# One kernel of attention and two expert layers: the hand-over order of its first phase written anew

## The chip, the cores and the metric

The kernel runs on one core of a Trainium2 chip. The metric is the device time of one execution in microseconds (us); lower is better. The core has five engines that each take their own instructions in order: TensorE (PE, with its weight loads as PEld), VectorE (DVE), ScalarE (ACT), GpSimd (POOL) and SyncE (SP), which here only issues transfers from HBM. They meet through semaphores.

## The reference, cut to what matters

Three stages follow one another: two kinds of attention that are added, then a mixture of 8 experts where each token goes to one, then a dense layer with a clipped quadratic in the middle.

```python
# q, k, v: (4, 8, 576, 64) float32
q_d, k_d, v_d = (a.reshape(B, H, 144, 4, D).mean(axis=3) for a in (q, k, v))
out_up = np.repeat(softmax(scale * q_d @ k_d.T) @ v_d, 4, axis=2)
mask = np.abs(pos[:, None] - pos[None, :]) < 4
out_local = softmax(np.where(mask, scale * q @ k.T, -1e9)) @ v
x = (out_up + out_local) as (2304, 512)
e = argmax(x @ w_gate)                 # one expert for each token
x = gate * (relu(x @ w1[e]) @ w2[e])   # (512 -> 1024 -> 512)
h = x @ w_in                           # (512 -> 2048)
out = where(h >= 1, h, where(h <= -1, 0, (h + 1)**2 / 4)) @ w_out
```

## The kernel before, in words

The first phase, up to about 120 us, computes both attentions for the four batches, the gating and the place of each token, and scatters the token rows into a buffer ordered by expert. The expert layer and the dense layer follow; they are the same in both kernels.

The first phase is a list of 526 short steps in the string `ORDER`. A loop walks it once and calls a function for each word, so the order of the words is the order in which every engine and the transfer queue get their instructions:

```python
    for step in ORDER.split():
        name, *args = step.split(".")
        ...
            fn, dve, other = CHOICE[name[:2]]
            ...
            fn(dve if name[2] == "v" else other, *args)
```

A word is a step and its indices. Where a third letter stands it chooses the engine: `v` is DVE, `p` POOL, `a` ACT. The steps that the prediction speaks of:

- Loads, all issued by SP in the order of the words: `q.b.i` (batch b of q in two pieces of 128x4x200 and 128x4x384 float32, 400 KB and 768 KB), `kr.b` (k for the pooled attention, 128x4x576, 1152 KB), `kb.n` (half a batch of k for the local attention), `vs.U` (v, 512 KB), `cs` (constants, 160 KB and 137 KB). A `kb` load is two transfers of 64x1184 (296 KB each) into 64 of the 128 partitions, into one of three buffers `kbd`, whose other quarters are zeroed by the memsets `mk`.
- Local attention, in 12 units U, three to a batch: `S.U` (scores on PE: one mask product, then 32 small float32 products, which the trace shows as 64 weight loads and 64 matmuls), `mx` and `sb` (row maximum, and its subtraction, on DVE), `ex` (exponential, ACT), `sm` (sum and reciprocal, DVE), `nm` (normalize, DVE or POOL), `tr` (transpose, DVE), `bd` (copies into a block layout `at`), `AV.U.g` (product with v, PE), `ac`/`ad`/`ap` (result into xT). `ma` zeroes the two `at` buffers.
- Pooled attention, batch by batch: `ka` and `pq` (pooling of k and q), `SD` (scores), `dm`, `dn`, `de`, `ds`, `dx` (softmax), `TD` (transposes on PE, copied into `adT` by `tc`), `vp` and `vc` (pooled v), `VD` (product), `vo`.
- Gating: `lg`, `ct`, `ch`, `ra`, `rk`, `rd` (logits, choice, place), `xt` and `xm` (rows transposed back and scaled by the gate), `xs` (scatter).
- `wu.i`: two products of 128x512 of ones by ones on PE, whose results nobody reads.

The functions of the half-partition load and of the scores:

```python
    def ld_kb(n):
        ...
        for h in range(2):
            SP.dma_start(out=kb[64 * h:64 * h + 64, h], in_=kT[b, x, 64 * h:64 * h + 64])
```

Of the kernel before, what the change touches and what calls it, by code (L numbers as in the profile page):

```python
# [56 lines left out]


ORDER = """
kr.0 mav.0 q.0.0 kap.0.0 m1 mkp.0.1 wu.0 wu.1 mkp.0.0 wu.2 mkv.1.1 wu.3 cs.0 q.0.1 kb.1 pqv.0.0 kap.0.1 ci mkp.2.0  # L60
pqv.0.1 kb.0 wu.4 mkv.1.0 q.1.1 wu.5 cm q.1.0 wu.6 me mdv.1 wu.7 S.0 SD.0.0 SD.0.1 cf wu.8 mx.0 wu.9 mkp.2.1 sb.0
wu.10 wu.11 wu.12 wu.13 S.1 dm.0.0.1 kr.1 mdv.0 dm.0.1.0 kb.2 dm.0.0.0 kb.3 dm.0.1.1 ex.0 vs.0 dn.0 cs.1 pqp.1.0 sm.0
nmv.0 wu.14 mx.1 tr.0 S.2 de.0.1.0 wu.15 kav.1.0 S.3 de.0.0.1 vs.1 pqp.1.1 de.0.1.1 mx.2 kap.1.1 sb.2 de.0.0.0 sb.1
ds.0 mx.3 SD.1.1 dm.1.1.1 ex.2 SD.1.0 dxp.0 bda.0.2 sb.3 dm.1.0.0 bda.0.3 dm.1.1.0 dm.1.0.1 ex.1 map.1 S.5 bda.0.0
sm.2 kb.4 TD.0.1 vs.2 sm.1 nmp.2 mx.5 bda.0.1 ex.3 dn.1 de.1.1.1 de.1.0.0 AV.0.0 tcv.0.1 TD.0.2 de.1.1.0 S.4 tca.0.2
AV.0.1 de.1.0.1 nmp.1 sm.3 tr.1 mx.4 tr.2 TD.0.0 bda.1.1 bdv.1.2 vp.0.0 acv.0.1 vp.0.1 q.2.0 aca.0.0 bdv.2.3 ds.1 cr
S.6 bda.1.0 bda.1.3 sb.4 kb.5 TD.0.4 mx.6 q.2.1 vca.0.0 kr.2 nmp.3 dxp.1 TD.0.3 ex.4 sb.5 AV.1.1 aca.1.1 sm.4 vca.0.1
AV.1.0 wg tca.0.3 bda.2.2 vs.4 TD.1.3 bda.2.1 vs.5 tcv.0.4 tr.3 tca.0.0 bda.2.0 aca.1.0 TD.1.1 nmv.4 bda.3.1 sb.6 vs.3
TD.1.4 pqv.2.0 VD.0.1 bdv.3.2 VD.0.0 TD.1.0 pqp.2.1 ex.5 TD.1.2 tr.4 tca.1.1 tca.1.4 AV.2.1 ex.6 AV.2.0 S.8 tca.1.0
sm.5 bda.3.0 tca.1.2 voa.0.0 kav.2.0 kav.2.1 acv.2.1 SD.2.0 bda.4.0 bdv.4.2 voa.0.1 tca.1.3 ce sm.6 bda.3.3 SD.2.1  # L70
mx.8 ap.1.0 ap.0.0 vp.1.1 bda.4.1 bda.4.3 vca.1.1 nmv.5 aca.2.0 dm.2.0.0 AV.3.1 aca.3.1 ap.0.1 ap.1.1 AV.3.0 tr.5
bda.5.0 nmp.6 S.7 lg.0 dm.2.1.0 dm.2.0.1 kr.3 sb.8 dm.2.1.1 mx.7 vp.1.0 aca.3.0 lov.0 ct.0 kb.6 dn.2 de.2.0.1 tr.6
de.2.1.1 vca.1.0 bdv.5.3 sb.7 AV.4.1 bdv.5.1 kav.3.0 de.2.1.0 AV.4.0 xt.2 xt.1 ap.2.1 ch.0 kav.3.1 de.2.0.0 ds.2 ra.0
VD.1.1 aca.4.0 vov.1.1 cx.0 dxv.2 xt.0 VD.1.0 ex.7 rk.0 kb.7 q.3.0 bda.5.2 q.3.1 gt.0 S.9 bdv.6.0 voa.1.0 TD.2.3
bda.6.1 aca.4.1 xma.0 rd.0 tca.2.3 AV.5.0 xma.2 ap.2.0 TD.2.2 TD.2.1 AV.5.1 sm.7 mx.9 ck acv.5.1 bda.6.3 ap.4.0
aca.5.0 pqp.3.0 pqp.3.1 S.10 SD.3.0 ex.8 ap.5.0 bda.6.2 vs.6 xs.0 ap.3.1 xma.1 tca.2.1 sm.8 TD.2.0 SD.3.1 mx.10
tca.2.2 AV.6.1 vs.7 nmv.7 ap.4.1 sb.9 dm.3.0.0 dm.3.1.0 S.11 dm.3.0.1 vs.8 ap.3.0 tr.7 ex.9 aca.6.1 dm.3.1.1 tca.2.0
dn.3 TD.2.4 vs.10 lg.1 sb.10 de.3.1.0 vp.2.1 loa.1 bdv.7.0 de.3.0.0 sm.9 ct.1 xs.2 vs.9 vp.2.0 ch.1 ra.1 tca.2.4
vcv.2.1 de.3.1.1 cx.1 bdv.7.3 ap.5.1 mx.11 bda.7.2 bdv.7.1 lg.2 vca.2.0 gt.1 nmp.8 loa.2 xt.5 AV.6.0 xt.3 aca.6.0 rk.1
tr.8 rd.1 xt.4 xma.5 de.3.0.1 xma.3 nmv.9 ct.2 VD.2.1 sb.11 bda.8.3 ch.2 ex.10 vp.3.0 tr.9 xs.1 xs.5 ds.3 xma.4  # L80
bda.8.1 ra.2 cx.2 bdv.8.0 xt.7 vs.11 xt.6 dxv.3 rk.2 vov.2.1 xs.3 VD.2.0 AV.7.1 vp.3.1 vov.2.0 vca.3.1 xs.4 AV.7.0
bda.8.2 gt.2 ad.7.1 xmv.6 sm.10 ap.6.1 TD.3.1 TD.3.0 xma.7 TD.3.2 ad.7.0 tca.3.1 ex.11 vca.3.0 AV.8.0 TD.3.4 rd.2
tcv.3.2 bda.9.0 tca.3.4 ap.6.0 lg.3 tca.3.0 bda.9.3 lov.3 nmp.10 xt.8 bdv.9.2 VD.3.0 xma.8 ad.8.0 tr.10 bda.9.1 ra.3
TD.3.3 AV.8.1 sm.11 ct.3 xs.6 voa.3.0 ad.8.1 tca.3.3 xs.7 AV.9.0 xs.8 VD.3.1 bda.10.1 bda.10.0 ch.3 bda.10.2 bda.10.3
nmv.11 voa.3.1 xt.10 cx.3 gt.3 aca.9.0 ap.9.0 AV.9.1 xt.9 rk.3 xt.11 tr.11 AV.10.0 aca.9.1 ap.9.1 rd.3 lg.4 xma.10
AV.10.1 xmv.9 ad.10.0 bda.11.0 xma.11 bdv.11.2 bdv.11.1 loa.4 bda.11.3 ct.4 ra.4 xs.10 ad.10.1 ch.4 cx.4 xt.12 xt.13
lg.5 rk.4 gt.4 xs.11 AV.11.1 AV.11.0 rd.4 xs.9 xma.13 loa.5 ad.11.1 ct.5 ad.11.0 xt.14 ch.5 lg.6 ra.5 xma.12 loa.6
xma.14 ct.6 rk.5 rd.5 xs.13 xt.15 cx.5 ra.6 ta gt.5 xt.17 xs.12 xs.14 xma.15 xt.16 ch.6 xs.15 cx.6 gt.6 rk.6 rd.6
xma.16 xma.17 tb xs.16 st ps xs.17
"""  # L90


# [1185 lines left out]
```

## Time and profile before

| | us |
|---|---|
| median of 3 runs | 760.63 (759.74 to 762.31) |
| the profiled execution's own time | 763.32 |
| its span in the profile | 761.5 |
| TensorE busy in the span | 729.6 |
| VectorE busy in the span | 524.0 |

The profile is of one execution. Its span runs from the first instruction to the last; the time of that execution is 1.8 us longer than the span. Busy time is the time in which an engine had an instruction in work.

### The profile page before, as it was taken

What the parts mean: (1) busy time and instruction counts of PE and PEld (TensorE: products, weight loads), DVE (VectorE), ACT (ScalarE), POOL (GpSimd) and SP (SyncE); (2) the same over time, 40 slices, a digit from 0 to 9 for tenths busy, and PEclk for the clock granted to TensorE, in tenths of its full rate; (3) what the DMA queues carried; (4) which work ended last, traced back from release to release, by engine and by line L of the source; (5) the groups of instructions that cost most, each with busy time, mean ns of one, the idle gap of its engine ahead of it and who ended that gap; (6) DMA issues with size and microseconds to landing.
All of it is one profiled execution on the core that took longest, in us unless ns stands there. A gap on an engine that the chain in (4) does not pass through costs nothing.

```text
span 761.5 us, 14260 instructions
## 1 busy us (share of the span) xinstructions
PE 729.6 (96%) x5520; PEld 655.9 (86%) x5521; DVE 524.0 (69%) x891; ACT 339.5 (45%) x697; POOL 254.2 (33%) x240
## 2 busy tenths in 40 slices
...
GB/s 284 248 235 318 113 86 185 261 210 177 143 209 202 200 217 246 202 174 51 29 55 28 56 56 28 57 29 56 28 56 28 56 0 1 1 42 41 42 42 83
DMA packets 47816, 87.09 MB, mean 114 GB/s; under 512 B 3084, under 2 KB 23948, under 8 KB 47736
## 3 DMA queue, kind: packets, MB, share of 16 engines
...
## 4 chain that ended last, share of the span: by engine, by line
PE 81%; issue 6%; DVE 4%; DMA 4%; POOL 2%; ACT 1%; SPq 1%; POOLq 0%; ACTq 0%; DVEq 0%
PE s L1065 24%; PE y L1163 15%; PE s L1003 13%; PE y L1020 13%; PE o L1163 8%; DMA kbd<-in_dram 2%; POOL out_dram L1183 1%; PE o L963 1%; DMA q_t<-in_dram 1%; PE o L400 1%; DMA xs_d<-xr,dst_all 1%; DMA xr<-xs_d 1%; PE s L400 1%; PE y L400 1%; PE o L524 1%
## 5 line engine op out<-in xcount | busy, mean ns | idle before, releaser
L1065 PE MATMUL s<-yT,wh 128*128 128x384 f32 x448 | 141.5, 339 | 0.0
L906 POOL TENSOR_SCALAR cvm<-cvm 128x512 f32<-128x512 f32 x32 | 52.9, 1654 | 243.9 <-ACT cvm L905 243.5
L1077 ACT CAST hh<-r 128x384 fp32r<-128x384 f32 x95 | 48.7, 513 | 161.0 <-DVE r L1073 161.0
L1072 DVE SCALAR_TENSOR_TENSOR r<-r 128x384 f32<-128x384 f32 x96 | 61.7, 643 | 64.9 <-ACT r L1071 63.7
L178 DVE TENSOR_TENSOR wl<-wraw,wh 128x1024 fp32r<-128x1024 f32 x64 | 82.2, 1303 | 22.5 <-ACT wh L177 22.0
L1071 ACT ACTIVATE r<-s,half 128x384 f32<-128x384 f32 x96 | 55.8, 581 | 87.9 <-PE s L1065 87.5
L1078 DVE TENSOR_TENSOR hl<-r,hh 128x384 fp32r<-128x384 f32 x95 | 56.4, 594 | 55.1 <-ACT hh L1077 53.9
L1065 PEld LDWEIGHTS s<-yT,wh 128*128 128x128 f32 x448 | 83.5, 188 | 4.8
L1065 PE MATMUL s<-yh,wh 128*128 128x384 f32 x256 | 85.9, 335 | 0.0
L1065 PE MATMUL s<-yh,wl 128*128 128x384 f32 x256 | 85.3, 333 | 0.0
L881 POOL TENSOR_TENSOR wl<-cvm,wh 128x512 fp32r<-128x512 f32 x32 | 50.8, 1587 | 99.7 <-ACT wh L880 88.7
L1163 PE MATMUL y<-wl,hh 128*128 128x512 f32 x189 | 74.1, 392 | 0.0
L1163 PE MATMUL y<-wh,hh 128*128 128x512 f32 x189 | 73.8, 391 | 0.0
L1020 PE MATMUL y<-hh,wh 128*128 128x240 f32 (+5 forms) x256 | 72.4, 303 | 0.0
L177 ACT CAST wh<-wraw 128x1024 fp32r<-128x1024 f32 x64 | 65.6, 1046 | 15.1 <-DMA wraw<-in_dram 10.6
L1020 PE MATMUL y<-hh,wl 128*128 128x240 f32 (+5 forms) x256 | 71.2, 298 | 0.0
L949 ACT ACTIVATE hh<-s 128x416 fp32r<-128x416 f32 (+7 forms) x64 | 27.9, 436 | 78.7 <-PE s L1003 78.7
L1163 PE MATMUL y<-wh,hl 128*128 128x512 f32 x189 | 59.5, 394 | 0.0
L950 DVE SCALAR_TENSOR_TENSOR hl<-s,hh 128x416 fp32r<-128x416 f32 (+7 forms) x64 | 31.1, 486 | 39.9 <-ACT hh L949 39.6
L1073 DVE TENSOR_TENSOR r<-s,r 128x384 f32<-128x384 f32 x96 | 53.5, 557 | 3.3
L1065 PEld LDWEIGHTS s<-yh,wh 128*128 128x128 f32 x256 | 48.0, 188 | 2.7
L1020 PEld LDWEIGHTS y<-hh,wl 128*128 128x128 f32 x256 | 48.3, 189 | 0.0
...
## 6 DMA issues: line engine op xcount, KB each, us to landing
...
```

The source lines that it names most:

```text
L177: ACT.copy(out=hi, in_=raw)
L178: DVE.tensor_tensor(out=lo, in0=raw, in1=hi.bitcast(F32), op=ALU.subtract)
L881: POOL.tensor_tensor(out=lo, in0=m, in1=hi.bitcast(F32), op=ALU.subtract)
L906: POOL.tensor_scalar(out=m, in0=m, scalar1=PAT_MIN * PAT_MIN, scalar2=None, op0=ALU.is_ge)
L1003: PE.matmul(out=h_ps[:, 0:m], lhsT=w[wi][:, o:o + 128], rhs=xhl[c][xi][:, 0:m], start=(n == 0), stop=(n == 11))
L1020: PE.matmul(out=y_ps[c][:, 0:m], lhsT=w[wi][:, o:o + 128], rhs=hl[xi][:, 0:m], start=(f == 0 and i == 0), stop=(f == 7 and i == 1))
L1065: PE.matmul(out=h_ps[:, 0:CAP], lhsT=w[wi][:, o:o + 128], rhs=yhl[j, c][xi], start=(n == 0), stop=(n == 11))
L1071: ACT.activation(out=r, in_=h_ps[:, 0:CAP], func=AF.Relu, scale=0.5, bias=half[:, 0:1])
L1072: DVE.scalar_tensor_tensor(out=r, in0=r, scalar=1.0, in1=r, op0=ALU.min, op1=ALU.mult)
L1073: DVE.tensor_tensor(out=r, in0=h_ps[:, 0:CAP], in1=r, op=ALU.max)
L1078: DVE.tensor_tensor(out=lo[:, 0:CAP], in0=r, in1=hi[:, 0:CAP].bitcast(F32), op=ALU.subtract)
L1163: PE.matmul(out=p, lhsT=gl[gi][:, 128 * t:128 * t + 128], rhs=w[wi][:, o + c:o + c + p.shape[-1]], start=(f % 4 == 0 and i == 0), stop=(f ...
```

## The change

Only the string `ORDER` changes: 521 words in place of 526, in another order, and with other engine letters on some. Sixteen `wu` words become eleven. Everything else is word for word the same, one line higher in the file (the string is a line shorter).

```diff
 ORDER = """
-kr.0 mav.0 q.0.0 kap.0.0 m1 mkp.0.1 wu.0 wu.1 mkp.0.0 wu.2 mkv.1.1 wu.3 cs.0 q.0.1 kb.1 pqv.0.0 kap.0.1 ci mkp.2.0
...
+mkv.2.1 m1 mkv.1.1 wu.0 mav.0 q.0.0 mdv.0 mkv.0.1 kb.0 wu.1 mkp.0.0 wu.2 cs.0 ci mav.1 cm S.0 q.0.1 me wu.3 mkv.2.0
...
```

The transfer queue (SP) at the start of the program, before. `kbd_100`, `kbd_101` and `kbd_102` are the three buffers of half-partition loads; `x2` is the pair of one `kb` step:

```order
L273 DMA kraw<-in_dram 128x4x576
L268 DMA q_t<-in_dram 128x4x200
L259 DMA cs<-in_dram 128x320
L268 DMA q_t<-in_dram 128x4x384
L287 DMA kbd_101<-in_dram 64x1184 x2
L287 DMA kbd_100<-in_dram 64x1184 x2
L268 DMA q_t<-in_dram 128x4x384
L268 DMA q_t<-in_dram 128x4x200
L273 DMA kraw<-in_dram 128x4x576
L287 DMA kbd_102<-in_dram 64x1184 x2
```

The same queue in the changed kernel:

```order
L267 DMA q_t<-in_dram 128x4x200
L286 DMA kbd_100<-in_dram 64x1184 x2
L258 DMA cs<-in_dram 128x320
L267 DMA q_t<-in_dram 128x4x384
L272 DMA kraw<-in_dram 128x4x576
L286 DMA kbd_101<-in_dram 64x1184 x2
L267 DMA q_t<-in_dram 128x4x200
L286 DMA kbd_102<-in_dram 64x1184 x2
L267 DMA q_t<-in_dram 128x4x384
L286 DMA kbd_100<-in_dram 64x1184 x2
```

The first `kraw` goes from first to fifth place, and the first pair of `kbd` from sixth to second; the second `kraw` stands behind all ten.

VectorE at the start of the program, before. `at_98` and `adp_109` are work buffers that are zeroed, `pt` and `qd` the pooling of q, `mx` the first row maximum:

```order
L302 MEMSET at_98 128x2048
L305 MEMSET kbd_101 64x1184
L452 TENSOR_TENSOR pt<-q_t 128x1152
L455 TENSOR_TENSOR qd<-pt 128x576
L305 MEMSET kbd_101 64x1184
L299 MEMSET adp_109 128x60x8
L367 TENSOR_REDUCE mx<-s_171 128x16
L371 TENSOR_TENSOR a_103<-s_171,mx 128x16x32
```

The same engine in the changed kernel:

```order
L304 MEMSET kbd_102 64x1184
L304 MEMSET kbd_101 64x1184
L301 MEMSET at_98 128x2048
L298 MEMSET adp_108 128x60x8
L304 MEMSET kbd_100 64x1184
L301 MEMSET at_99 128x2048
L304 MEMSET kbd_102 64x1184
L366 TENSOR_REDUCE mx<-o_136 128x16
L370 TENSOR_TENSOR a_103<-o_136,mx 128x16x32
L277 TENSOR_TENSOR kraw<-kraw 128x1152
L280 TENSOR_TENSOR k_d<-kraw 128x576
L304 MEMSET kbd_101 64x1184
```

Memsets moved here from POOL, the pooling of q went to POOL, and the first pooling of k (`kraw`, `k_d`) came from POOL.

TensorE from the scores of unit 5 on (`S.5`, `TD`, `AV`, `TD`, `S.4`, `AV`), before:

```order
L359 MATMUL y_441<-kbd_100,q_t 32x64 x32
L503 MATMUL s_481<-ident,adp_108 96x128 x4
L400 MATMUL y_503<-at_98,v_s 64x96 x8
L503 MATMUL y_514<-ident,adp_108 96x128 x4
L350 LDWEIGHTS identb
L350 MATMUL s_521<-maskb,identb 128x512
L359 MATMUL s_521<-kbd_102,q_t 32x64 x16
L359 MATMUL s_521<-kbd_100,q_t 32x64 x16
L400 MATMUL o_556<-at_98,v_s 64x96 x8
```

The same piece of work in the changed kernel, from `S.2` on (`S.2`, `S.5`, `S.4`, `AV`, `TD`, `vp`, `TD`, `AV`):

```order
L358 MATMUL y_359<-kbd_101,q_t 32x64 x32
...
L358 MATMUL y_393<-kbd_100,q_t 32x64 x32
L349 LDWEIGHTS identb
L349 MATMUL o_433<-maskb,identb 128x512
L358 MATMUL o_433<-kbd_102,q_t 32x64 x16
L358 MATMUL o_433<-kbd_100,q_t 32x64 x16
L399 MATMUL y_474<-at_98,v_s 64x96 x8
L502 MATMUL s_486<-ident,adp_108 96x128 x4
L410 MATMUL y_491<-v_s,cs 32x512 x3
L502 MATMUL o_506<-ident,adp_108 96x128 x4
L399 MATMUL s_519<-at_98,v_s 64x96 x8
```

Three scores now stand next to one another, with no transposes or products between them, and the scores of the second batch's pooled attention (`SD.1`), which stood ahead of `S.5`, stand behind all of this.

## Rows read from the trace of the kernel before

**Rows 1.** Busy time by stretch: stretch, its length, busy (instructions) by engine, PEclk, DMA, GB/s.

```profile
18.00:33.50 15.50, 14.34 (x378) 9.15 (x376) 14.90 (x29) 11.01 (x43) 10.63 (x7) 1.00 1.02 291
33.50:45.00 11.50, 8.16 (x139) 4.89 (x139) 5.42 (x13) 5.21 (x16) 4.07 (x3) 0.70 0.75 214
45.00:84.00 39.00, 38.65 (x754) 27.68 (x751) 37.21 (x76) 31.86 (x90) 21.30 (x23) 1.00 0.73 243
84.00:118.80 34.80, 32.84 (x470) 24.97 (x468) 26.81 (x88) 23.06 (x53) 19.76 (x31) 1.00 0.30 108
...
134.60:761.50 626.90, 620.54 (x3662) 582.01 (x3662) 425.71 (x653) 263.45 (x488) 184.96 (x148) 1.00 0.29 94
```

**Rows 2.** The chain that ended last, 30 to 60 us: start, length, what.

```profile
33.52 3.34 issue
36.86 1.29 PE s L359 x37
...
40.64 1.81 PE o L411 x6
...
46.48 0.66 PE o L400 x16
...
48.58 1.18 PE y L524 x16
...
56.53 1.02 PE y L411 x6
```

**Rows 3.** DVE's waits, 20:40 and 40:64: total, times, longest.

```profile
DVE mx L367 <- PE s L359: 3.0, 1, 3.0
...
DVE mx L367 <- PE y L359: 2.9, 1, 2.9
```

**Rows 4.** Busy time from 0 (columns as rows 1); instruction queue at 34.0:34.5 and 0:38.5.

```profile
0.00:29.30 29.30, 18.91 (x356) 10.32 (x357) 19.32 (x28) 9.36 (x33) 15.78 (x22) 1.00 0.96 289
...
0.00:33.50 33.50, 23.11 (x473) 13.38 (x474) 23.42 (x37) 13.06 (x48) 19.98 (x25) 1.00 0.97 284
...
q8 instruction: 1, 0.02, 13.8%
...
q8 instruction: 4, 0.07, 0.8%
```

**Rows 5.** Busy time, while full-width loads run and while half-partition loads run.

```profile
4.00:8.00 4.00, 0.00 (x0) 0.00 (x0) 0.27 (x1) 0.00 (x0) 1.58 (x1) 1.00 1.07 382
11.00:15.00 4.00, 4.00 (x11) 1.38 (x10) 3.66 (x3) 0.00 (x0) 3.80 (x9) 1.00 1.01 230
```

**Rows 6.** The timeline, first instructions: start, length, what, [idle before <-releaser].

```profile
1.28 1.76 DVE L302 MEMSET at<- 128x2048 f32 x1 [1.16 <-PEq L1266]
...
6.42 2.61 POOL L278 TENSOR_TENSOR kraw<-kraw 128x1152 f32<-128x1152 f32 x1 [5.55 <-DMA kraw<-in_dram]
...
16.98 0.69 DVE L367 TENSOR_REDUCE mx<-s 128x16 f32<-128x512 f32 x1 [1.20 <-PE s L359]
...
25.95 1.10 PE L359 MATMUL y<-kbd,q_t 128*32 128x64 f32 x64 [0.96 <-DMA kbd<-in_dram]
```

**Rows 7.** DVE by line and form, 0 to 119 us: busy, mean ns, idle before.

```profile
L385 DVE TENSOR_TENSOR a<-a,sm 128x512 f32<-128x512 f32 x6 | 4.5, 752 | 0.0
...
L278 DVE TENSOR_TENSOR kraw<-kraw 128x1152 f32<-128x1152 f32 x3 | 4.0, 1321 | 0.0
...
L452 DVE TENSOR_TENSOR pt<-q_t 128x1152 f32<-128x1152 f32 x2 | 2.7, 1350 | 6.3 <-DMA q_t<-in_dram 6.3
L305 DVE MEMSET kbd<- 64x1184 f32 x2 | 2.1, 1045 | 0.5 <-issue 0.5
...
L701 DVE TENSOR_SCALAR xr<-s,gt 128x512 f32<-128x512 f32 x1 | 0.7, 742 | 0.0
...
L512 DVE COPY adT<-y 96x512 f32<-96x512 f32 x1 | 0.7, 677 | 0.0
...
L514 DVE COPY adT<-o 96x256 f32<-96x256 f32 x1 | 0.4, 356 | 0.0
```

More of the change, by code (lines that the diff above doesn't have):

```diff
@@ L59 @@
 ORDER = """
-kr.0 mav.0 q.0.0 kap.0.0 m1 mkp.0.1 wu.0 wu.1 mkp.0.0 wu.2 mkv.1.1 wu.3 cs.0 q.0.1 kb.1 pqv.0.0 kap.0.1 ci mkp.2.0
[L61 to L89, printed above, removed]
+mkv.2.1 m1 mkv.1.1 wu.0 mav.0 q.0.0 mdv.0 mkv.0.1 kb.0 wu.1 mkp.0.0 wu.2 cs.0 ci mav.1 cm S.0 q.0.1 me wu.3 mkv.2.0
@@ new lines @@
+kr.0 pqp.0.0 kb.1 mx.0 wu.4 sb.0 wu.5 kav.0.0 wu.6 ex.0 wu.7 pqp.0.1 kav.0.1 mkv.1.0 SD.0.0 dm.0.0.0 dm.0.0.1 SD.0.1
+dm.0.1.0 q.1.0 dm.0.1.1 dn.0 sm.0 kb.2 de.0.0.1 de.0.1.0 S.1 q.1.1 mx.1 kb.3 wu.8 cs.1 nmp.0 sb.1 wu.9 ex.1 tr.0 S.3
+pqp.1.0 de.0.0.0 bdv.0.0 de.0.1.1 bda.0.1 bdv.0.2 vs.0 cf wu.10 mx.3 vs.1 sm.1 ce ds.0 nmv.1 S.2 S.5 mx.2 sb.3 sb.2
+bda.0.3 dxp.0 S.4 mx.4 kr.1 tr.1 ex.2 AV.0.1 sm.2 TD.0.4 vp.0.0 bda.1.1 bdv.1.0 ex.3 tcv.0.4 q.2.0 sb.4 bda.1.2
+pqp.1.1 TD.0.2 bda.1.3 ex.4 nmp.2 sm.3 tr.2 AV.0.0 bda.2.0 TD.0.3 kap.1.0 q.2.1 bda.2.2 acv.0.0 tca.0.2 bda.2.1 mx.5
@@ new lines @@
+kap.1.1 TD.0.0 nmp.3 sb.5 bda.2.3 kb.4 sm.4 tca.0.3 AV.1.1 ex.5 AV.1.0 TD.0.1 aca.0.1 SD.1.0 vs.2 tca.0.0 nmp.4 sm.5
+aca.1.1 kr.2 aca.1.0 SD.1.1 tr.3 dm.1.0.0 vs.3 pqp.2.0 dm.1.0.1 vca.0.0 S.6 bda.3.1 wg vp.0.1 dm.1.1.0 dm.1.1.1 AV.2.1
+bda.3.2 bda.3.0 kb.5 bda.3.3 tca.0.1 dn.1 AV.2.0 mx.6 vcv.0.1 VD.0.1 de.1.0.0 tr.4 de.1.1.0 sb.6 kav.2.0 acv.2.1
+pqp.2.1 bdv.4.2 kav.2.1 nmp.5 de.1.1.1 voa.0.1 bdv.4.0 VD.0.0 ck vov.0.0 bda.4.1 AV.3.1 vs.5 tr.5 AV.3.0 SD.2.0
+de.1.0.1 cr aca.3.1 mdv.1 dm.2.0.0 SD.2.1 bda.5.0 S.7 aca.3.0 ap.1.1 S.8 dm.2.1.0 aca.2.0 ap.0.1 bda.5.1 dm.2.0.1 kr.3
@@ new lines @@
+dm.2.1.1 mx.7 vs.4 ds.1 dxv.1 ap.1.0 bda.5.3 dn.2 ap.0.0 bda.5.2 kap.3.0 lg.0 AV.5.1 de.2.0.0 de.2.1.0 sb.7 lov.0 xt.0
+TD.1.4 mx.8 ap.2.1 de.2.0.1 tcv.1.4 vs.6 TD.1.3 ex.7 TD.1.2 vp.1.0 ex.6 tcv.1.3 ct.0 sb.8 ra.0 tcv.1.2 q.3.1 ch.0
+bda.4.3 de.2.1.1 q.3.0 TD.1.0 ds.2 AV.5.0 aca.5.1 cx.0 kap.3.1 TD.1.1 vs.8 vp.1.1 pqp.3.0 tca.1.1 vcv.1.0 gt.0 vca.1.1
+sm.6 acv.5.0 xt.2 xt.1 tca.1.0 sm.7 xmv.2 AV.4.1 VD.1.0 pqp.3.1 rk.0 vs.7 rd.0 VD.1.1 voa.1.0 xma.0 ex.8 kb.6 voa.1.1
+ap.2.0 ap.3.1 xma.1 SD.3.1 SD.3.0 nmv.6 ap.3.0 dm.3.1.0 dm.3.0.1 aca.4.1 vp.2.1 vs.11 kb.7 dm.3.1.1 dm.3.0.0 dn.3 lg.1
@@ new lines @@
+AV.4.0 S.9 de.3.1.0 dxv.2 ap.5.1 loa.1 tr.6 ra.1 xs.0 ct.1 aca.4.0 xt.3 xs.2 vcv.2.1 vp.2.0 ch.1 de.3.1.1 xt.5
+de.3.0.1 cx.1 rk.1 de.3.0.0 S.11 vs.10 mx.9 nmp.7 gt.1 TD.2.0 xs.1 rd.1 xmv.3 bda.6.1 ap.4.0 sm.8 ap.4.1 bda.6.0 sb.9
+ap.5.0 tr.7 xs.3 vca.2.0 mx.11 S.10 mx.10 lg.2 ra.2 bda.6.2 xt.4 xma.5 loa.2 ct.2 ds.3 TD.2.4 bda.6.3 ch.2 xma.4
+tca.2.0 cx.2 xt.8 TD.2.2 AV.6.0 rk.2 tca.2.4 tca.2.2 TD.2.3 gt.2 TD.2.1 nmp.8 xma.8 tr.8 sb.11 tcv.2.1 xs.5 xs.4 ex.9
+bda.7.1 AV.6.1 tca.2.3 xt.6 vp.3.1 VD.2.1 rd.2 dxp.3 sm.9 aca.6.1 xs.8 bdv.7.2 xma.6 sb.10 bdv.8.3 bda.8.0 xs.6 ex.11
@@ new lines @@
+sm.11 nmv.11 bdv.8.1 TD.3.0 VD.2.0 bdv.7.0 bda.7.3 TD.3.1 vov.2.0 TD.3.4 AV.7.1 voa.2.1 ex.10 aca.6.0 ap.6.0 nmv.9
+ap.6.1 tcv.3.4 TD.3.3 bda.8.2 vs.9 AV.8.1 tca.3.0 xt.7 AV.7.0 AV.8.0 xma.7 sm.10 tr.9 nmv.10 tca.3.3 bdv.9.2 ad.7.1
+TD.3.2 ad.8.1 ad.7.0 xs.7 bdv.9.1 bda.9.0 tr.10 bda.9.3 ad.8.0 tca.3.1 vp.3.0 tca.3.2 tr.11 AV.9.1 AV.9.0 vca.3.0
+aca.9.1 lg.3 vca.3.1 bdv.11.3 bda.10.2 aca.9.0 bdv.10.1 lov.3 VD.3.0 ct.3 bda.11.2 VD.3.1 bdv.10.3 ra.3 xt.9 vov.3.0
+voa.3.1 ap.9.1 ch.3 bdv.10.0 rk.3 AV.10.0 cx.3 gt.3 ap.9.0 xt.10 bda.11.0 bda.11.1 xt.11 xma.9 lg.4 rd.3 loa.4 AV.11.1
```

3 lines of the change are left out of this document (added).

## The prediction, written before the changed kernel ran

> **What bounds the kernel now.** I read the busy time by stretch first [rows 1]. The last 626.9 us, behind 134.6, belong to the expert and dense layers, with PE busy for 620.5; the change touches nothing there, so I carry them over. From 118.8 to 134.6 the last scatters land and the first expert's rows come back: 15.8 us that hang on the last scatter alone and shift with it. What can change is the time up to 118.8.
>
> There VectorE is the engine to watch. It is busy for 14.90 of 15.5 us from 18 to 33.5 and for 37.21 of 39 from 45 to 84, but only for 5.42 of 11.5 between, a hole of 6.1 us. From 84 to 118.8 PE leads (32.84 of 34.8) and DVE idles 8.0.
>
> The hole is explained by the chain [rows 2]: at 33.52 PE stops for 3.34 us in the middle of one unit's scores, 27 of 64 matmuls done, "issue": it waited for nothing that the profile shows. DVE waits 3.0 us for those scores and 2.9 us for the next ones [rows 3]. In that stretch the granted clock averages 0.70 [rows 1], a mixture of its two levels, 1.2 and 2.4 GHz: behind the pause six products of the pooled v took 1.81 us where later ones took 1.02 [rows 2].
>
> What was PE waiting for? By 33.5 it had 947 records (473 matmuls, 474 weight loads), and up to 38.5 the instruction queue had brought four packets of 16 KB, one of them in the half microsecond after 34.0, in the pause [rows 4]. 947 over four is 237 records a packet. The mark before, 711, lies at 29.3 (713 records). So PE ran through one packet in 4.2 us, and the next was there only 36.86 - 29.3 = 7.5 us after the mark. That the packet is late because it queues among the loads is my reading; the rows show only the coincidence.
>
> On instruction packets the Trainium skill (Runtime: NRT & Kernel Launch, section Instruction fetch mechanics) says that the next 16 KiB is fetched while the present one is executed, and that the crossing is mostly hidden. The packet size agrees with the trace; "mostly hidden" does not hold at 33.52, where 3.34 us stood open. By the page such a pause would cost nothing in the changed kernel; that is the first rival below.
>
> **The change, part by part.**
>
> *Earlier start, +6.8 us.* The first row maximum starts at 16.98 [rows 6]. Loads run at 382 GB/s full width and at 230 GB/s in half-partition pairs [rows 5]. The first load of before (1152 KB, 1.18 MB) is used at 6.42 [rows 6]; 1.18 / 0.382 = 3.1 us, so the queue counts from 3.3. In the new order: q.0.0 4.4, kb.0 7.0, cs.0 7.5, q.0.1 9.5, kr.0 12.6, kb.1 15.3, q.1.0 16.3, kb.2 19.0, q.1.1 21.0, kb.3 23.7. S.0 can thus run from about 8. DVE has its seven memsets first: from 1.28, four of 1.045, two of 1.76, a short one of 0.46, and gaps of 0.1 each, which end at 10.2. The memsets, not the loads, set the first maximum: 10.2.
>
> *More DVE work behind it, -2.2 us.* Against before, behind the first maximum: one memset more (+1.05), one first half of k's pooling fewer (-1.32), one of q's fewer (-1.35), one normalization fewer (-0.75), three adT copies more (0.68 and two of 0.36), two v_d copies of the same 96x512 (1.36), two row scalings (1.48), one block copy (about 0.35, taken like the 0.36 ones): sum +2.2 [rows 7]. What left DVE lies on POOL, which is busy for 21.3 of 39 us in the densest stretch [rows 1]; were that cover gone, each normalization there would hold up the transpose behind it on DVE.
>
> *Fewer wu words, 0.* Nobody reads them. Before the first scores PE has nothing else to do. Without the cover they could let the clock fall, which is priced below.
>
> *DVE's hole goes, +6.7 us.* The 6.1 us of 33.5 to 45, and the 0.6 us of 18 to 33.5 [rows 1], belong to the old order; what takes their place follows.
>
> *Waits for early loads, -1.2.* Behind `sb.0`, at about 11.6, DVE pools kr.0, which is used from 12.6: 1.0. Waiting for SD.0 I put at 0.2.
>
> *Scores of unit 4 on their load, -1.9 (0 to 4.2).* S.5 needs kb.3. DVE reaches the maximum of unit 4 after 25 instructions: at the 0.51 mean of [rows 1] (14.90/29) 12.8 us; most of them are passes of 0.68 over 128x512, so I take 0.60, 15.1, hence 10.2 + 15.1 + 1.2 = 26.5. S.5 and S.4 take 1.10 for the scores [rows 6] and some 0.3 for the mask product each, so S.4 is done at 23.7 + 2.8 = 26.5: no wait. But by the same sum the kb.2 of before lands at 24.1, and S.3 got it at 25.95 [rows 6]: 1.9 us late, and I take that lateness here too.
>
> *Instruction packets, -3.3 (0 to 8.6).* Counting records along the new order, the marks 237, 474, 711 and 947 fall just into S.1, near the end of S.3, in the second half of S.5 and between TD.0.2 and AV.0.0. By the loads PE reaches them at about 16.4, 20.5, 24.6 and 30.3. The steps are 4.1, 4.1 and 5.7 us, as dense as the 4.2 that stalled. If no packet is late the cost is 0, as at the two marks ahead in before. If each takes 7.5 us the fourth mark comes at 16.4 + 22.5 = 38.9, 8.6 late. I take one late packet: 7.5 - 4.2 = 3.3, since one of three was late before.
>
> *Small waits of DVE, -0.8.* From 26.5 to 45 I let DVE idle at the share of 18:33.5 and 45:84, 2.4 of 54.5 us, times 18.5.
>
> *A heavier tail on PE, -1.0 (0 to 2).* Behind the last transpose of the local softmax PE has two AV (0.66), two VD (1.18), one logits step, one small and three larger transposes more than before, some 6 us (AV and VD from [rows 2]). DVE alone would end the phase earlier than PE by up to 2 us.
>
> Sum: 6.8 - 2.2 + 6.7 - 1.2 - 1.9 - 3.3 - 0.8 - 1.0 = **3.1 us** faster. The profiled execution took 763.32 (span 761.5 and 1.8 around it), so its like would take 760.2; the median of the three runs is 760.63, and 760.63 - 3.1 = **757.5 us**. I forecast for the median.
>
> **The rivals.**
>
> *No late packet.* The page's rule, as a mechanism of this kernel: the packets come in time, since kb.2, q.1.1 and kb.3 pace PE anyway. Then the 3.3 is not paid: 6.4 us faster, 754.2. For it: two of the first three marks of before passed without a pause. Against it: the third did not, at the same pace and under the same kind of load.
>
> *The hole comes back.* The new order only moves it: one late packet and behind it the slow clock, as before. The half-speed stretch cost PE about 0.65 on the scores (37 matmuls in 1.29 where 64 take 1.10) and 0.8 on the pooled v [rows 2, 6], and DVE the second wait of 2.9 [rows 3]. Forecast minus that second wait: 0.2 us faster, 760.4. For it: marks as close as before. Against it: PE's work there is scores that wait on loads, so a late packet can hide behind a late load.
>
> *Slower: two or three late packets in the burst.* S.1, S.3, S.2, S.5 and S.4 stand almost next to one another, some 650 records, and every one is wanted by DVE at once. If all three packets take 7.5 us, 8.6 us are lost in place of 3.3, and behind a pause the clock falls, another 1.5: 3.1 - 5.3 - 1.5 = 3.7 slower, 764.3. It decides once the packets together cost over 6.4 us. For it: half-partition loads, among which the packet of before was late, fill the queue through this whole stretch. Against it: the three marks of before under load lost 3.3 in all.
>
> **How the numbers follow.** The forecast holds with 0.5, no late packet 0.12, the hole comes back 0.23, slower 0.15. Runs of this kernel lie within 759.74 to 762.31, so 0.3%, 2.3 us, is about what a measurement can tell from no change; the edges are 758.35 and 762.9. The forecast's own range is 755.5 to 759.5, and I put 0.13 of its 0.5 above 758.35. Faster: 0.37 + 0.12 = 0.49. Same: 0.13 + 0.23 = 0.36. Slower: 0.15. The range reaches from the rival without late packets, 754.0, to just over the upper edge, 763.0; beyond lie about 0.08 below and 0.12 above.
>
> **What would show it.** Right: first maximum near 10.2; S.5 starting at 23.7 to 25.6; one "issue" pause of about 3 us on PE inside S.3, S.5 or just ahead of AV.0.0; DVE's idle time from 18 to 45 at 5 to 6 us with less than half of it in one piece; the last scatter 3 us earlier; the stretch behind it as long as before. Wrong: the loads land later than the two rates say, so that the maxima wait on transfers; or several pauses on PE before 35 us; or the head start is there at 45 us and is lost behind 84, where PE leads.

## The result, and the profile after

The changed kernel takes 769.1 us (median of 4 runs, 764.52 to 770.72), the kernel before 760.18 us beside it (4 runs, 759.68 to 762.31): ratio 1.0099, 95% interval 1.0072 to 1.0125. It is slower by 1%; 757.5 was predicted. The profiled execution took 768.16 us (span 766.4), 4.84 more than that of before. The medians are 8.9 apart, since the profiled execution of before is a long one of its kind and that of after is not; the traces therefore show about half of the loss directly, and the ratios of the experiments have to say the rest.

Two rows of the busy time by stretch answer to [rows 1] (columns as there; lines of the changed kernel are numbered one lower):

```profile
18.00:33.50 15.50, 9.73 (x331) 6.81 (x330) 8.82 (x19) 6.72 (x27) 7.12 (x4) 0.86 1.05 330
33.50:45.00 11.50, 11.36 (x146) 7.91 (x144) 9.66 (x20) 8.92 (x18) 8.91 (x6) 0.89 0.73 182
```

The hole of before is filled: PE is busy for 11.36 of 11.5 us where it was 8.16. But the stretch ahead of it now has the hole, PE 9.73 and DVE 8.82 where they had 14.34 and 14.90. To see where time is lost it helps to cut at places where both kernels stand alike, and to end at PE's first product of the expert layer, 134.61 us before and 138.81 after. First the kernel before, then the changed one:

```profile
0.00:15.00 15.00, 5.77 (x14) 2.06 (x16) 6.90 (x6) 2.05 (x5) 8.65 (x18) 1.00 0.90 262
15.00:45.00 30.00, 25.50 (x598) 16.22 (x597) 21.94 (x44) 16.22 (x58) 15.40 (x10) 0.89 0.93 268
45.00:60.00 15.00, 14.88 (x306) 11.74 (x306) 14.36 (x26) 12.98 (x29) 5.82 (x6) 1.00 0.71 253
60.00:115.00 55.00, 53.55 (x880) 38.23 (x868) 47.83 (x126) 39.97 (x109) 32.89 (x44) 1.00 0.48 161
115.00:134.61 19.61, 9.38 (x86) 5.67 (x82) 7.22 (x40) 4.89 (x10) 6.48 (x17) 0.74 0.57 184
```

```profile
0.00:15.00 15.00, 7.89 (x81) 3.57 (x82) 10.82 (x11) 2.48 (x5) 5.05 (x15) 1.00 0.88 252
15.00:45.00 30.00, 23.05 (x503) 16.11 (x507) 21.11 (x43) 15.64 (x45) 16.03 (x10) 0.89 0.93 266
45.00:60.00 15.00, 12.57 (x348) 9.62 (x339) 13.61 (x26) 14.68 (x55) 7.28 (x8) 1.00 0.94 317
60.00:115.00 55.00, 49.84 (x766) 35.26 (x764) 48.54 (x109) 33.85 (x86) 32.84 (x40) 1.00 0.42 134
115.00:138.81 23.81, 16.13 (x174) 10.82 (x174) 12.22 (x60) 6.16 (x13) 9.41 (x23) 0.78 0.68 223
```

PE's busy time is nearly the same, 109.1 and 109.5 us. Of the 4.2 us 3.8 are idle time of PE: 2.1 us less up to 15 us, then 2.5 more up to 45, 2.3 more up to 60 and 3.7 more up to 115, and 2.6 less behind. Behind these marks the changed kernel takes another 0.7 us longer (627.6 and 626.9), which makes up the 4.9 between the spans. Row two of before also says what I had read past: of PE's 4.5 idle us there 3.34 are the one pause. From 15 to 115 us PE was idle for 6.1 of 100 in the kernel before and DVE for 15.9, so PE, not DVE, is the engine with the least room in this phase.

The idle time has names. The chain of the changed kernel, 20 to 32 us (start, length, what):

```profile
20.69 0.75 PE s L358 x37
21.44 2.30 issue
23.75 0.64 PE s L358 x27
...
26.49 0.62 PE y L358 x33
27.11 3.02 issue
30.14 1.08 PE y L358 x30
```

These are pauses in the middle of `S.3` and `S.5`, like the one of [rows 2]; two more follow, 0.37 us at 51.53 and 2.04 at 56.04. PE has then 442, 697, 1458 and 1712 records, matmuls and weight loads together. The busy time up to the first pause shows the count, 220 and 222:

```profile
0.00:21.40 21.40, 12.80 (x220) 6.88 (x222) 16.79 (x22) 4.69 (x17) 6.09 (x16) 1.00 0.94 261
```

These counts are 188 plus 1, 2, 5 and 6 times 254 or 255. The pause of before, at 947 [rows 4], lies at 188 plus 3 times 253. From this I take it that packets end every 254 records or so and that the first end stands at 188, not at 237 and its multiples. The pauses make 7.7 us in all, 3.3 before.

Between 60 and 115 us nearly all of PE's idle time is two waits for the one-hot comparison of `ch`. DVE and POOL in the timeline, and PE behind them (start, length, what, [idle before <-releaser]):

```profile
78.17 0.18 DVE L574 TENSOR_REDUCE m<-c 128x3 f32<-128x24 f32 x1
78.38 3.25 DVE L575 TENSOR_TENSOR oh_all<-c,m 128x24 bf16<-128x24 f32 x1
...
78.01 1.02 POOL L629 DMA_INDIRECT xs_d<-xr,dst_all  x1 [0.17 <-ACT adp L485]
...
79.09 2.50 POOL L428 TENSOR_TENSOR xT<-xT,xd 128x384 f32<-128x384 f32 x3
...
81.69 0.19 PE L599 MATMUL y<-oh_all,onesb 128*128 128x16 bf16 x2 [2.48 <-DVE oh_all L575]
```

An operation on 24 numbers a partition that takes 0.18 us elsewhere takes 3.25, and ends when POOL's run ends at 81.59. At 88.04 it happens again, 3.33 us, until POOL's multiplication of `adp` is done at 91.31. A third one, 1.76 us at 64.86, does not hold PE up.

Last, the transition. PE's warm-up products between the phases, the first transposes of expert rows and the first products, before and after:

```profile
128.70 3.03 PE L832 MATMUL y<-onesb 128*128 128x512 bf16 x8
132.55 0.36 PE L963 MATMUL o<-ident,xr 96*128 96x96 f32 x2 [0.82 <-DMA xr<-xs_d]
134.61 1.62 PE L1003 MATMUL s<-xh,wh 128*128 128x368 f32 x4 [0.43 <-issue]
```

```profile
131.50 0.82 PE L831 MATMUL y<-onesb 128*128 128x512 bf16 x3 [0.21 <-issue]
135.68 0.55 PE L962 MATMUL o<-ident,xr 96*128 96x96 f32 x2 [3.36 <-DMA xr<-xs_d]
138.81 1.86 PE L1002 MATMUL s<-xh,wh 128*128 128x368 f32 x4
```

After an idle time of 3.36 us in place of 0.82 the granted clock is 0.50 from 135.6 to 141 (1.2 GHz), where before had 1.00. From the first transpose to the first product it takes 3.13 us in place of 2.06, and the first 24 products take 5.74 in place of 4.97. Together that is 1.8 us.

### The profile page after: what moved, and what is told of

Same layout as the page of the kernel before. It is cut to its first block, busy times and chain, and to the rows that moved or that the text cites. A ratio compares the mean times of both kernels' runs of the same rounds, so it can differ in the third digit from the quotient of the medians.

```text
span 766.4 us, 14247 instructions
## 1 busy us (share of the span) xinstructions
PE 730.7 (95%) x5510; PEld 658.4 (86%) x5511; DVE 531.7 (69%) x898; ACT 336.1 (44%) x689; POOL 255.4 (33%) x241
## 4 chain that ended last, share of the span: by engine, by line
PE 83%; issue 6%; DVE 4%; DMA 3%; POOL 2%; ACT 1%; SPq 0%; POOLq 0%; ACTq 0%; DVEq 0%
PE s L1064 24%; PE y L1162 15%; PE s L1002 13%; PE y L1019 13%; PE o L1162 8%; DMA kbd<-in_dram 2%; POOL out_dram L1182 1%; PE o L962 1%; PE y L399 1%; DVE oh_all L575 1%; DMA xr<-xs_d 1%; PE o L399 1%; PE y L358 1%; PE y L466 0%; PE s L523 0%
```

## The experiments

Ratios are to the kernel before on the same chip, with their 95% interval; the changed kernel's is 1.0099. Where only words of `ORDER` move, the diff shows the cut.

### Which part of the order loses

**ab34** and **ba46**: one order up to a word, what is left in the other.

```
 ab34: changed order ... bda.1.2 pqp.1.1 | rest as before
 ba46: order before ... bda.2.2 vs.4     | rest as changed
```

> The order of the changed kernel up to its 34 us (through the fifth scores), then all other steps in the order of before. Start theory (what is lost is lost in the packed scores of the first 34 us): about as slow as the changed kernel, 766 to 770. Rest theory (the middle and the tail lose it: the one-hots that wait, the third pause at 56 us, the heavier tail): 757 to 762.

> The order of before up to its 46 us, its pause included, then all other steps in the order of the change. Start theory: about as fast as before, 759 to 762. Rest theory: 764 to 769.

Measured: ab34 764.63 us, 1.0054 (1.0034 to 1.0074); ba46 767.65, 1.0089 (1.0071 to 1.0106). Both parts lose. ab34, which falls between its two expectations, has the pause in `S.3` (2.6 us) and two shorter ones (0.5 and 0.9); ba46 has that of before (3.3) and a 3.25 us comparison with PE waiting 2.5 for it.

**ab46**, **ab66** and **ba66**: cuts at other places.

> The changed kernel's order up to about 47 us (its first 153 steps), and what is left in the order of the kernel before; the other way round from ba46. If the changed kernel lost time in two separate places, its start (about 3 us) and its middle (about 6 us, as ba46 showed): 763.5 to 765.5 us here, and no comparison of 3 us, since those stand in the middle of the changed order. If the start alone is the cause and the middle only passes it on: 767 to 770. If the start costs nothing: 760.5 to 762.

> The changed kernel's order up to about 66 us (its first 256 steps), then what is left in the order of the kernel before. TensorE's idle time up to 66 us is 2.6 us more in the changed kernel than before, and behind it 1.6 us more in all to the second phase. If the two add up: 2.5 to 3.5 us over the kernel before here, and the waits for oh_all of 2.5 us each are gone. If the loss is made behind 66 us: within 1.5 us of the kernel before. If the mixed order has waits of its own at its seam, as ab46 had one of 6.6 us for adp: over 5 us more, and then the run tells nothing of the sum.

> The other way round: the order of the kernel before up to about 66 us (its first 257 steps), then the changed order. If what is lost in front of 66 us and behind it adds up: 1.5 to 5 us over the kernel before, with one pause of 3.3 us at record 947 and one or two comparisons of 3.2 us that TensorE waits for. If the changed order behind 66 us is as good as the old one: within 1 us of the kernel before.

Measured: ab46 772.74, 1.0121 (1.0082 to 1.0161); ab66 769.31, 1.0067 (1.0044 to 1.0090); ba66 772.16, 1.0090 (1.0063 to 1.0118). ab46 and ba66 missed every expectation. PE's longest wait between 45 and 60 us in ab46 shows one reason, and ba66 has the like between 62 and 122 (engine, line, waited for: total, times, longest):

```profile
PE s L506 <- POOL adp L499: 6.6, 1, 6.6
```

```profile
PE s L470 <- POOL qd L458: 3.0, 1, 3.0
PE y L603 <- DVE oh_all L579: 2.5, 1, 2.5
```

These two mixed orders have waits behind their seam that neither order has. ab66 has none like them (PE's longest wait from 60 to 122 us is 0.8): with the four pauses of the changed start in it, 7.7 us, and every comparison at 0.18 us or less, it loses 0.67%, 5.1 us, where 2.5 to 3.5 were expected. The parts don't add up, 0.67% and 0.90% making more than the whole, so halves say that there is more than one cause, not what each costs. The remedies below leave the order whole.

### Instruction packets

**fewer_wu**: the words `wu.3` to `wu.10` taken out.

> The changed kernel without the eight warm-up steps wu.3 to wu.10 (16 matmuls and 16 weight loads less, all before the scores of unit 2). If TensorE stops where a packet of instructions ends: the pauses come at the same counts of records, 442 and 697, so 16 matmuls later in the program: in the scores of unit 3 after 53 of 64 matmuls where it was 37, in those of unit 5 after 49 where it was 33; the time stays at 767 to 771 us, since a packet is as late as before. If the pauses belong to a place in the program or to a moment: still after 37 and 33 matmuls, or at 21.4 and 27.1 us in whatever stands there. If the warm-ups carried the clock: a granted clock under 1.0 before 18 us, and a time over 771.

Measured: 769.53, 1.0075 (1.0054 to 1.0095). The scores of units 3 and 5, the piece ahead of each pause:

```profile
20.49 0.97 PE L362 MATMUL s<-kbd,q_t 128*32 128x64 f32 x51
...
26.61 0.89 PE L362 MATMUL o<-kbd,q_t 128*32 128x64 f32 x49 [1.07 <-DMA kbd<-in_dram]
```

51 and 49 matmuls where they were 37 and 33. (51 and not 53: `wu.10` stands behind `S.3` on PE, so only 14 matmuls had gone by then.) The first pause comes again at 442 records:

```profile
0.00:21.40 21.40, 10.83 (x220) 6.70 (x222) 16.38 (x21) 4.18 (x15) 5.78 (x16) 1.00 0.95 261
```

The second comes again at 697. The pauses hang on the count of instructions, not on a place in the program.

**depth2** and **depth3**: loads from `q.1.0` to `vs.3` held until the load two, or three, before has landed, by a transfer of one number on SP's queue (the diff shows depth3).

```diff
+    def hold(kind, *a):
+        src = ...        # one element of an earlier load's tile
+        SP.dma_start(out=hold_t[0:1, n:n + 1], in_=src)
...
-q.1.0 dm.0.1.1 dn.0 sm.0 kb.2 ... q.1.1 mx.1 kb.3
+hd.0.0.1 q.1.0 dm.0.1.1 dn.0 sm.0 hd.2.0 kb.2 ... hd.1.1 q.1.1 mx.1 hd.0.1.0 kb.3
```

> The changed kernel, but from the seventh load to the fourth of v each load waits until the load two places ahead has landed (a transfer of one element that reads it stands before each), so that the transfer queue holds two loads and not eight. Queue theory (a packet is late because it queues behind the loads already issued): the gap from the mark to the packet falls from 6.4 to 6.9 us to under 5, the two pauses of TensorE before 31 us shrink from 5.3 us together to under 2, and the time falls by 2 to 5 us unless the loads themselves land later. Rival (the packets take 6 to 7 us however few loads are ahead): pauses of 2 us and more stay, the time is the same or longer by what the loads lose.

> The changed kernel with a small transfer on SyncE's queue ahead of each load from q.1.0 to vs.3, which reads what the load three before it has brought, so that at most three loads are under way. If packets of instructions come late because they stand in the same DMA engines as many loads: they are recorded earlier than 21.0, 27.5 and 34.5 us, TensorE's pauses without a cause before 35 us fall from 5.3 us to under 2, waits for loads grow by 2 to 5 us (by less than with two loads under way), and the time is 766 to 772. If packets are late for another reason: pauses of 2.3 and 3.0 us as before.

Measured: depth2 773.14, 1.0163 (1.0129 to 1.0198); depth3 770.97, 1.0130 (1.0059 to 1.0201). PE's waits from 8 to 60 us in depth2:

```profile
PE y L422 <- DMA v_s<-in_dram: 5.1, 2, 2.9
...
PE y L489 <- POOL k_d L303: 3.8, 1, 3.8
PE s L381 <- DMA kbd<-in_dram: 2.7, 1, 2.7
...
PE y L381 <- DMA kbd<-in_dram: 1.6, 1, 1.6
```

Not one "issue" is left there, and the first three packets are recorded at 17.5, 24.5 and 30.5 us where they were at 21.0, 27.5 and 34.5 (18.5, 24.0 and 29.5 in depth3; the queue was read in half microseconds). That PE came later to the packet's end does not explain it: at 17 us it had 195 records in both. The changed kernel up to 17.1 us and its instruction queue from 21.0 to 21.5, then depth2 up to 17.0 and from 17.5 to 18.0:

```profile
0.00:17.10 17.10, 8.95 (x97) 4.63 (x98) 12.59 (x13) 2.48 (x5) 5.05 (x15) 1.00 0.91 256
q8 instruction: 1, 0.02, 13.7%
```

```profile
0.00:17.00 17.00, 9.33 (x97) 4.68 (x98) 12.66 (x13) 2.49 (x5) 5.06 (x15) 1.00 0.83 235
q8 instruction: 1, 0.02, 17.4%
```

With fewer loads under way the packets come sooner: this shows that they were late behind the loads, which the prediction had as a coincidence. The loads are late instead, so nothing is won.

**early_hold**: the holds of depth3, only up to `kr.1`.

> The changed kernel with the small holding transfers of depth3 only ahead of the loads from q.1.0 to kr.1, and none behind. If late packets are what costs the start and waits for v_s behind 45 us are what depth3 paid: pauses without a cause before 40 us under 3 us (7.3 to 9 without holding), TensorE's idle time up to 60 us 1 to 3 us less than the changed kernel's 16.5, and a ratio to the kernel before of 1.003 to 1.008. If the loads are late instead: idle time up to 60 us as before or more, ratio 1.009 to 1.015.

Measured: 767.15, 1.0078 (1.0052 to 1.0104). Pauses 1.3 us, PE idle for 15.2 us up to 60 instead of 16.5; waits for `kbd` of 2.4 and 2.3 us take most of it back. As expected of the packets, though the interval overlaps the changed kernel's, so a gain is not shown.

**before_hold**: the same remedy in the kernel before, for the three loads in flight at its one pause.

```diff
-kb.4 TD.0.1 vs.2 sm.1 ... vp.0.1 q.2.0
+hd.3.1 kb.4 TD.0.1 hd.4.1 vs.2 sm.1 ... vp.0.1 hd.1.4 q.2.0
```

> The order of the kernel before, with three small transfers on SyncE's queue, so that kb.4, vs.2 and q.2.0 each wait until the load two before has landed. The kernel before has one pause of TensorE without a cause, 3.34 us at record 947, while these loads fill the queue. If the packet stands behind the loads: the pause falls under 1.5 us and the kernel takes 757.5 to 760 us in place of about 761. If the held loads come too late instead: waits for kbd, v_s or q_t of 1 to 4 us on TensorE behind 36 us, and 761 to 765. If the packet's lateness has nothing to do with loads: the pause stays at 3.3 us, and 760 to 762.

Measured: 761.54 us where the kernel before had 764.77 on this chip, 0.9966 (0.9953 to 0.9979), 12 and 19 runs: faster than both kernels. PE's waits between 20 and 60 us, and its first products of the expert layer, which start 3.5 us earlier than before:

```profile
PE y L381 <- DMA kbd<-in_dram: 1.8, 1, 1.8
PE y L381 <- DMA q_t<-in_dram: 1.0, 1, 1.0
PE y L433 <- DMA v_s<-in_dram: 1.0, 1, 1.0
```

```profile
131.13 4.97 PE s L1025 x24
```

The pause is gone altogether, and the granted clock is 1.00 from 33.5 to 45 us where it averaged 0.70 [rows 1]. The held loads (`q_t` and `v_s`) cost PE 2.0 us; the wait for `kbd`, at 26.57, ends ahead of the first holding transfer (1.0 us in the kernel before). The gain, 0.34%, is 2.6 us in this comparison.

### The one-hot comparisons

**oh_scalar**: another form of the comparison.

```diff
-        DVE.tensor_tensor(out=oh_all[:, g0:g0 + n], in0=c1, in1=m2.unsqueeze(2)..., op=ALU.is_equal)
+        for g in range(n):
+            DVE.tensor_scalar(out=oh_all[:, g0 + g], in0=c1[:, g], scalar1=m2[:, g:g + 1], ..., op0=ALU.is_equal)
```

> The changed kernel, but the one-hot of the gating is written token group by token group with a per-partition scalar in place of one operation with two tensors in SBUF. Port theory (VectorE's 3.25 and 3.33 us one-hots waited for GpSimd's run of operations over the port that the two share, and cost the changed kernel 6 us): no one-hot longer than 0.5 us, the time 3 to 6 us under the changed kernel's 769, near 764. Packet theory (the late instruction packets of TensorE cost it all, the one-hots stand in time that is idle anyway): the one-hots may be short, the time stays within 2 us of 769.

Measured: 772.86, 1.0168 (1.0131 to 1.0204). The three small comparisons take 3.51 us together at 80.64: held up like the one. The first theory missed: this form, with a scalar from SBUF in place of a second tensor, does not avoid it.

**clear_ports** and **ports_dve**: POOL's work moved away in time, or given to DVE.

```diff
 clear_ports, order of POOL:
-ap.4.0 ap.4.1 ap.5.0 xs.3 ... dxp.3 xs.8
+xs.3 ap.4.0 ap.4.1 ap.5.0 ... xs.8 dxp.3
 ports_dve:
-nmp.7 ... nmp.8 ... dxp.3
+nmv.7 ... nmv.8 ... dxv.3
-        add_xd(POOL, U, gi, x_of(U, gi))
+        add_xd(DVE if (U, gi) in ((4, 0), (4, 1), (5, 0)) else POOL, U, gi, x_of(U, gi))
```

> The changed kernel with five steps of its order moved, nothing else: the three additions to xT on GpSimd behind the next row scatter, the multiplication of adp on GpSimd behind a later scatter, and one transposition of rows with its eviction a little later, so that no long run of GpSimd stands beside the two one-hot comparisons that took 3.25 and 3.33 us. If VectorE is held up there by GpSimd's run: both comparisons take at most 1.3 us, TensorE's waits for oh_all fall from 5.5 us to under 2, and the kernel takes 764 to 766.5 us where the changed one takes 769.1. If the comparison is slow by itself, or the time is only found again elsewhere: 3.2 us each as before, or 768 to 770 us.

> The changed kernel with six of GpSimd's steps between 73 and 92 us given to VectorE (three additions to xT, the multiplication of adp in step dx.3, and nm.7 and nm.8), about 4 us more work for VectorE, and GpSimd left with the scatters there. If GpSimd's runs hold VectorE up: no VectorE instruction over 1.2 us longer than its like between 76 and 92 us, TensorE's waits for oh_all fall from 5.5 us to under 1.5, and the kernel takes 765 to 767.5 us, 1.5 to 4 below the changed one. If VectorE is full in this stretch, so that what it does itself costs what it waited: 768 to 771.

Measured: clear_ports 770.74, 1.0103 (1.0061 to 1.0145); ports_dve 771.26, 1.0083 (1.0052 to 1.0114). The 3 us comparisons are gone in both, and the time is not. In clear_ports PE waits 2.1 us for `adp` and 1.7 for `xT` from POOL, and a copy on DVE takes 3.11 where its like take 0.35. In ports_dve, 60 to 115 us:

```profile
PE y L403 <- DVE at L397: 1.6, 1, 1.6
PE s L362 <- issue: 1.4, 4, 0.5
PE y L362 <- issue: 1.2, 3, 0.4
```

Moving work moved the wait here; neither run says what the comparisons cost.

**oh_psum**: only the place of two small operands changes.

```diff
-        l3 = ap2.tile([128, n, E], F32, tag="l3", name="l3")
+        l3 = T["ct", k][:, 384:384 + n * E].rearrange("p (g e) -> p g e", e=E)
...
-        c1 = ap2.tile([128, n, E], F32, tag="c1", name="c1")
+        c1 = T["ct", k][:, 448:448 + n * E].rearrange("p (g e) -> p g e", e=E)
```

> The changed kernel with the sums and the coded maxima of the one-hot step written into the unused columns of the PSUM bank that the step holds anyway, so that the subtraction and the one-hot comparison each read one operand from PSUM and one from SBUF, in place of two from SBUF. Order, engines and work are the same. If a VectorE instruction with two SBUF operands is held up by GpSimd's run: both comparisons fall from 3.25 and 3.33 us to under 0.5 with GpSimd's instructions still beside them, TensorE's waits for oh_all from 5.5 us to under 1.5, and the time falls by 2 to 5 us, to a ratio of 0.999 to 1.004 with the kernel before (the changed kernel's is 1.010). If the comparisons are held up by something else: 3.2 us as before. If they are short and the time stays (1.008 or more): the middle has another limit, and the waits only showed it.

Measured: 766.1, 1.0064 (1.0041 to 1.0087). The timeline of DVE and POOL:

```profile
79.45 1.25 DVE L575 SCALAR_TENSOR_TENSOR o<-lgx,cs 128x24 f32<-128x24 f32 x1
...
80.96 0.18 DVE L578 TENSOR_TENSOR oh_all<-o,m 128x24 bf16<-128x24 f32 x1
88.21 0.18 DVE L578 TENSOR_TENSOR oh_all<-y,m 128x24 bf16<-128x24 f32 x1
```

```profile
80.81 1.01 POOL L633 DMA_INDIRECT xs_d<-xr,dst_all  x1 [0.17 <-issue]
...
88.17 0.96 POOL L633 DMA_INDIRECT xs_d<-xr,dst_all  x1 [0.21 <-DVE m L577]
```

Both comparisons take 0.18 us in the middle of a POOL instruction, so the comparison was held up by having both operands in SBUF. The Trainium skill (SBUF — State Buffer, section SBUF: two separate sides) has the rule: VectorE and GpSimd share one pair of ports, and the one that starts first, a VectorE instruction with two SBUF inputs (against a GpSimd one that reads SBUF) or the GpSimd one, keeps it for the whole instruction. The trace agrees and adds that the wait can last through a scatter and three additions in a row, 3.25 us. Two inputs are not the only case: in the kernel before, a copy on DVE with one input, in SBUF, takes 2.54 us at 79.02 beside POOL's run, where its like take 0.35.

The time fell less than expected (0.999 to 1.004), and the interval overlaps the changed kernel's. PE still waits 1.9 us for `oh_all` and 0.7 for `gt` between 60 and 115 us, and one step ahead of the first comparison, whose two inputs stayed in SBUF, is now the one that is held up (1.25 us in the first line, 0.18 in the changed kernel).

**before_hold_psum**: both remedies in the kernel before.

> before_hold with the one-hot step's operands in PSUM as in oh_psum. TensorE's one wait for oh_all there is 1.0 us, at the end of the phase, where the last rows go out. If that wait is GpSimd's doing: 0.5 to 1 us less than before_hold, ratio to the kernel before 0.994 to 0.996. If it is the length of the chain of small steps: no change, 0.996 to 0.998.

Measured: 760.18, 0.9994 (0.9977 to 1.0010). Slower than both expectations, and no gain from the PSUM operands shows. The gain of before_hold itself does not show on this chip either, although the pause at record 947 is gone here too. PE waits 2.5 us for the held loads where it waited 2.0 in before_hold, and stops for 1.0 us at record 1959, again a packet's end by the count. Why the two comparisons differ stays open: holding gave 0.34% in one and nothing clear of noise in the other.

### The start of the second phase, and all together

**both**: early_hold and oh_psum in one kernel. **warm24**: the changed kernel with a longer warm-up between the phases. **all3**: the two of them together.

```diff
     for t in hb + yb:
-        for _ in range(2):
+        for _ in range(4):
             PE.matmul(out=t, lhsT=onesb, rhs=..., start=True, stop=True)
```

> early_hold and oh_psum in one kernel. If late packets and held-up comparisons are the two causes and add up: a ratio to the kernel before of 0.996 to 1.003. If the loss is made elsewhere: 1.006 or more.

> The changed kernel with 24 warm-up matmuls between the phases where it has 12, nothing else. They cost nothing where TensorE waits for the first rows anyway (3.36 us in the changed kernel, 12 matmuls at full clock take 2.6 us). If the gap lets the clock fall, and that is part of the loss: granted clock 1.00 through the transposes and the first matmuls, transposes in about 1.6 us in place of 3.1, the first 24 matmuls in 4.97 in place of 5.74, 1.5 to 3 us less, a ratio to the kernel before of 1.006 to 1.008. If the clock isn't what the gap costs, or the warm-ups come into the way of the transposes: 1.009 or more.

> The kernel of both with the 24 warm-up matmuls. If late packets, held-up comparisons and the cold start of the second phase are what the changed kernel lost: a ratio to the kernel before of 0.999 to 1.003, about 9 in 10 of the loss won back. If the longer warm-up only delays transposes that were no longer cold: 1.004 to 1.007, as without it.

Measured: both 764.86, 1.0049 (1.0030 to 1.0068); warm24 765.53, 1.0066 (1.0046 to 1.0086); all3 763.36, 1.0038 (1.0023 to 1.0053). both falls between its two expectations. In warm24 the timeline of PE is

```profile
133.25 3.41 PE L835 MATMUL y<-onesb 128*128 128x512 bf16 x15 [1.15 <-issue]
138.53 1.62 PE L1006 MATMUL s<-xh,wh 128*128 128x368 f32 x4 [0.43 <-issue]
139.98 0.83 PE L1006 MATMUL s<-xh,wl 128*128 128x368 f32 x4
```

and the granted clock 1.00 from 132 to 141 us: the first products run at full speed again. The first transposes start only when the longer warm-up is done, at 136.50 in place of 135.68, so part of the 1.8 us is given back. The three remedies together win back 0.61 of the 0.99%, and the intervals of all3 and of the changed kernel do not overlap. Those of all3 and both do, so what the warm-up adds there is not shown. all3 fell short of what I expected, 0.999 to 1.003, by a little.

## Why the prediction was wrong

- **"There VectorE is the engine to watch"**: this failed first. The two gains, +6.8 and +6.7, count DVE's work and DVE's holes; but PE was idle for only 6.1 us between 15 and 115, and while its work takes as long as before a new order can win no more than that between these marks. before_hold points the same way: it takes PE's one pause away and was faster in one of two comparisons (in the other the operands in PSUM came with it), where DVE's whole new order was slower.
- **Earlier start, +6.8**: the first maximum came at 11.26, not 10.2. The scores started at 9.26 instead of about 8, since the constants for the mask were used only from 8.14 (I had them landed at 7.5), and they took 1.94 us where I used 1.10; 1.94 is also what `S.4` took at 31.68, where the granted clock is 0.50. More to the point, for PE the head start was worth 2.1 us at 15 us, and at 25 us both kernels stood level: 501 matmuls and weight loads after, 521 before, by then.
- **Waits for early loads, -1.2**: the right size. DVE waited 1.1 us for `kr.0` where I had 1.0, though PE waited 2.1 for the pooled k. **Scores of unit 4, -1.9**: `kb.2` landed at 20.55 where I had 19.0, near the lateness that I took, but PE waited only 0.45 us for it; the pauses, not the loads, then held the scores up.
- **Instruction packets, -3.3 (0 to 8.6)**: the term that was mis-sized. The marks were wrong (237 apart instead of 254 behind a first 188): I divided 947 by four packets, but the fourth came at 38.36, when the pause was over [rows 2]. And "one late packet" became four pauses of 7.7 us, 4.4 more than before, within the bounds but at their far end. In six profiled executions with the same first 300 steps they make 7.7 to 10.0 us. Several pauses on PE before 35 us were among the signs of being wrong, and the rival "slower: two or three late packets in the burst" had the mechanism, though not the size (764.3). Two things differ from before, and no run separates them. One is density: `S.3`, `S.2`, `S.5` and `S.4` stand close together with about 128 records each, and the 255 records between the first two pauses ran in 3.4 us (23.75 to 27.11), where packets were recorded 6.5 to 7 us apart. The other is that packets were later: from PE's record 188, 442 and 697 to the packet's record it took 2.6, 2.1 and 5.5 us before, and 4.0, 6.1 and 7.5 after.
- **"No late packet"** and the sentence of the Trainium skill that the crossing is mostly hidden (Runtime: NRT & Kernel Launch, section Instruction fetch mechanics): pauses of 2.0 to 3.3 us stood open while loads filled the queue; in depth2, with two loads under way, none did.
- **Not foreseen: comparisons that POOL holds up.** PE waited 5.5 us for them where it had waited 1.1. The trace of before had shown the like, out of PE's way: a copy of 2.54 us on DVE that takes 0.35 otherwise.
- **A heavier tail, -1.0**: PE's last one-hot products ended 5.2 us later (123.77 and 118.55), with the losses above in it. The last scatter ended 3.4 us later (126.25 and 122.87) and the first transposes started 3.1 us later, so up to there the stretch did "hang on the last scatter". Not foreseen was that the warm-up, which started almost when it did before (127.29 and 127.04), ends too early for these rows and no longer keeps the clock up: 1.8 us.

What stays open: 0.38% in all3, about 2.9 us. Part of it are the loads that holding makes late (PE waits 6 us for `kbd` and `v_s` there); how much is the changed order itself was not separated. The comparisons of executions as a whole also show more loss than the traces (8.9 us between the medians, 4.8 between the profiled executions), and the rest has no place in a trace. What each remedy is worth alone, 0.2 to 0.35%, is inside the others' intervals; only their sum is shown.
